# Decode attention with a gated dense branch: key tiles of four heads in 32 KB rows, and a softmax per tile among the key transposes

## The chip, the cores and the metric

One core of a Trainium2 chip. The metric is device time in microseconds, the median of several executions. Engines: PE (matrix products), DVE (VectorE), ACT (ScalarE), POOL (GpSimd), SP (which issues nearly all DMA transfers). "PEclk" is the clock granted to PE, 1.00 being full speed.

## The reference, cut to what matters

One token. Branch A: 32 query heads over 16 key/value heads, a window of 4,096 cached positions, 128 elements per head. Branch B: a dense layer of 576 to 4,608 to 576 with GELU. A sigmoid gate mixes them.

```python
W = min(4096, max(256, Sk // 4))                       # 4096
q = (x @ wq)                                           # 32 heads of 128
k = jnp.repeat(k_cache[:, :, Sk - W:, :], 2, axis=1)   # 16 heads, each for two query heads
v = jnp.repeat(v_cache[:, :, Sk - W:, :], 2, axis=1)
p = softmax(einsum("bhqd,bhkd->bhqk", q, k) * 128**-0.5)
a = einsum("bhqk,bhkd->bhqd", p, v).reshape(1, 1, 4096) @ wo
b = gelu(x @ w1 + b1) @ w2 + b2
return g * a + (1 - g) * b                             # g = sigmoid(sum(x * gate_w))
```

Keys and values are 16.8 MB each and the weights 20.0 MB: 53.6 MB are read once, for one row of output.

## The kernel before

Four large buffers A to D take turns: w1 in B, wq in A, then keys in C, D, B, A, w2 in B, values in C, D, A, C, wo in D. A load can be issued only when the work on its buffer's former content is done, and SP issues in one fixed order. Keys come two heads at a time, in rows of 16 KB (64 blocks of 64 positions x 2 heads = 128 partitions). VectorE transposes them, PE forms the scores of all 16 heads into one tile, then one large softmax runs, then the value products.

```python
s_ps = ps_s.tile([P, SL * 32], FP32, name="s_ps")            # 128 x 2048, all heads
for g in range(NG):                                          # 4 tiles
    k_t = big.tile([P, 2, SL, Dh], BF16, name="k_t", tag="CDBA"[g])
    for f in range(2):                                       # 2 loads each
        h0 = HB * g + 2 * f
        src = A_k_cache[0, h0 : h0 + 2, Sk - W : Sk, :].rearrange(
            "b (k c) d -> k b (c d)", k=P // 2)
        nc.sync.dma_start(out=k_t[:, f, :, :].rearrange("p c d -> p (c d)"), in_=src)
        ...  # two transposes on VectorE, 16 products into s_ps
...  # maximum over everything, two small products, negm
for f in range(2):
    for b in range(HB):
        nc.scalar.activation(out=p_t[:, cs, :, b], in_=..., func=ACT.Exp,
                             bias=negm[:, b : b + 1], scale=SCALE, accum_out=...)
    nc.vector.transpose(out=pt[:, cs, :]..., in_=p_t[:, cs, :, :]...)
w2_t = big.tile([P, NF, D], BF16, name="w2_t", tag="B")
nc.sync.dma_start(out=w2_t[:, 0:NJ, :], in_=w2_src[:, 0])    # first half of w2
...
for g in range(NG):
    v_t = big.tile([P, NCK, Dh], BF16, name="v_t", tag="CDAC"[g])
    nc.sync.dma_start(out=v_t[:].rearrange("p c d -> p (c d)"), in_=src)   # 32 KB rows
    for c in range(NCK):
        v_last = nc.tensor.matmul(o_ps[:, 8 * g : 8 * g + 8, 0], lhsT=v_t[:, c, :], ...)
...  # wo (2 loads), second half of w2 (3 loads), output products, one row out
```

## Time and profile before

| | before |
|---|---|
| time, median of 4 runs | 132.57 us (132.45 to 132.85) |
| span of the profiled run | 131.1 us |
| packets of the data queue, share of 16 DMA engines | 96.3% |
| last weights landed (end of the DMA step in the chain) | 128.24 us |
| from there to the end of the span | 2.9 us |

The bounds are read in the prediction. Two more lines of the page before show the two costliest pieces of work that the change touches (line, engine, operation, output<-input, forms, count; then busy us, mean ns; then idle time before them and who ended it):

```profile
L399 DVE STREAM_TRANSPOSE kt<-k_t 128x2048 f32<-128x2048 f32 x16 | 36.0, 2290 | 6.7 <-DMA k_t<-in_A_k_cache_dram 6.7
L451 ACT ACTIVATE p_t<-s_ps,negm 128x512 bf16<-128x512 f32 x8 | 9.7, 1415 | 44.6 <-DVE negm L442 44.6
```

VectorE idles 6.7 us for keys, so it keeps up with them. ScalarE's softmax is a block of 9.7 us after everything.

### The profile page before, as it was taken

Reading aid. Unit: us, or ns where it says so; the run is one execution under the profiler, and the core shown is the slowest. Engines: PE = TensorE matmul, PEld = TensorE weight load, DVE = VectorE, ACT = ScalarE, POOL = GpSimd, SP = SyncE. Lnnn points to the kernel's source line nnn. Section 1 sums busy time; section 2 is a strip of 40 time slices with the busy share of each in tenths; the row PEclk is TensorE's granted clock in tenths of the full one; section 3 lists DMA queues with packets and bytes.
Section 4 is the critical chain, followed back from the end, with each engine's and each line's share of the span. In section 5 each row is a group of like instructions: output and inputs, shape, how many; then the busy total and the mean of one; then the engine's idle time right before and its main releaser. Section 6 shows DMA issues by size and latency. Waiting matters only on the chain.

```text
span 131.1 us, 2372 instructions
## 1 busy us (share of the span) xinstructions
PE 77.1 (59%) x1126; PEld 44.5 (34%) x1062; DVE 50.3 (38%) x48; ACT 12.9 (10%) x25; POOL 5.9 (4%) x25
## 2 busy tenths in 40 slices
PE   0210899975599968768769220005935740997573
PEld 0110779975111211111111010005834730954441
DVE  0232000042988988988986720735000000010001
ACT  3000000003000000000000039950000000000001
POOL 5029000000000000000000000000000000000000
PEclk9999999999999999999999985555555555558999
DMA  8999899899999999999999999999989999999980
GB/s 290 421 394 496 382 461 421 367 440 420 425 415 440 420 425 435 425 430 425 436 430 489 420 410 450 420 410 450 465 380 435 460 405 392 416 444 415 397 326 20
DMA packets 3044, 53.75 MB, mean 410 GB/s; under 512 B 342, under 2 KB 346, under 8 KB 732
## 3 DMA queue, kind: packets, MB, share of 16 engines
q1 hardware_dynamic: 3026, 53.61, 96.3%
q8 instruction: 8, 0.13, 0.4%
q10 hardware_dynamic: 10, 0.01, 0.0%
HBM read 53.62 MB, written 0.00 MB: 409 GB/s over the span
## 4 chain that ended last, share of the span: by engine, by line
DMA 67%; PE 12%; DVE 8%; ACT 8%; issue 3%; SPq 1%; DVEq 0%
DMA k_t<-in_A_k_cache_dram 26%; DMA w_t<-in_B_w_dram 20%; DMA wq_t<-in_A_wq_dram 20%; ACT p_t L451 7%; PE o_ps L495 5%; DVE kt L399 3%; PE q_ps L356 3%; DVE pt L459 2%; DVE m L421 2%; PE s_ps L409 1%; PE y_ps L291 1%; SPq L508 1%; PE t_ps L475 0%; DVE out_row L537 0%; SPq L510 0%
## 5 line engine op out<-in xcount | busy, mean ns | idle before, releaser
L399 DVE STREAM_TRANSPOSE kt<-k_t 128x2048 f32<-128x2048 f32 x16 | 36.0, 2290 | 6.7 <-DMA k_t<-in_A_k_cache_dram 6.7
L409 PE MATMUL s_ps<-kt,qz_flat 128*128 128x512 bf16 x128 | 32.7, 404 | 8.5 <-DVE kt L399 8.5
L495 PE MATMUL o_ps<-pt,v_t 128*128 128x8 bf16 x512 | 14.5, 168 | 10.4 <-DMA v_t<-in_A_v_cache_dram 7.1
L409 PEld LDWEIGHTS <-qz_flat 128*128 128x128 bf16 x64 | 6.5, 101 | 34.1 <-issue 34.1
L495 PEld LDWEIGHTS <-v_t 128*128 128x128 bf16 x512 | 14.3, 105 | 10.7 <-DMA v_t<-in_A_v_cache_dram 7.3
L451 ACT ACTIVATE p_t<-s_ps,negm 128x512 bf16<-128x512 f32 x8 | 9.7, 1415 | 44.6 <-DVE negm L442 44.6
L318 PEld LDWEIGHTS <-w_t 128*128 128x128 bf16 x162 | 10.2, 165 | 1.0 <-issue 1.0
L318 PE MATMUL h_ps<-x,w_t 128*128 128x2 bf16 x162 | 10.4, 202 | 0.0
L513 DVE TENSOR_TENSOR om<-o_ps,rgh 128x128 bf16<-128x128 f32 x1 | 0.3, 292 | 24.0 <-PE o_ps L495 24.0
L475 PE MATMUL t_ps<-ls,ones 128*128 128x32 f32 x2 | 0.6, 396 | 12.7 <-DVE ls L473 12.7
L459 DVE STREAM_TRANSPOSE pt<-p_t 128x2048 bf16<-128x2048 bf16 x2 | 4.6, 2312 | 7.4 <-ACT p_t L451 7.4
L291 PE MATMUL y_ps<-w_t,gt 128*1 128x288 bf16 x72 | 6.7, 345 | 1.1 <-DMA w_t<-in_B_w_dram 1.1
L327 DVE COPY hacc<-h_ps 128x36 f32<-128x36 f32 x1 | 0.2, 196 | 14.9 <-PE h_ps L318 14.9
L291 PE MATMUL y_ps<-wo_t,ov 128*1 128x288 bf16 x64 | 4.4, 286 | 2.3 <-DMA wo_t<-in_A_wo_dram 2.3
L537 DVE CAST out_row<-y_ps 1x288 bf16<-1x288 f32 x1 | 0.4, 446 | 12.3 <-PE y_ps L291 12.3
L475 PEld LDWEIGHTS t_ps<-ls,ones 128*128 128x128 f32 x2 | 0.5, 310 | 12.8 <-issue 12.8
L291 PEld LDWEIGHTS <-gt 128*1 128x1 bf16 x72 | 3.5, 96 | 3.5 <-issue 1.5
L356 PE MATMUL q_ps<-x,wq_t 128*128 128x2 bf16 x144 | 4.0, 166 | 1.0 <-DMA wq_t<-in_A_wq_dram 1.0
L536 ACT CAST out_row<-y_ps 1x288 bf16<-1x288 f32 x1 | 0.4, 389 | 42.3 <-PE y_ps L291 42.3
L356 PEld LDWEIGHTS <-wq_t 128*128 128x128 bf16 x144 | 3.9, 104 | 1.1 <-DMA wq_t<-in_A_wq_dram 1.1
L291 PEld LDWEIGHTS <-ov 128*1 128x1 bf16 x64 | 2.8, 84 | 3.6 <-issue 2.5
L306 PE MATMUL h_ps<-ident,rows 2*128 2x2 bf16 x18 | 1.3, 198 | 4.2 <-DMA rows<-in_B_b_dram 4.2
(65 smaller groups left out, 27.9 us busy)
## 6 DMA issues: line engine op xcount, KB each, us to landing
k_t<-in_A_k_cache_dram SPq DMA_DIRECT2D x8, 2048.0 KB, 30.4
v_t<-in_A_v_cache_dram SPq DMA_DIRECT2D x4, 4096.0 KB
w_t<-in_B_w_dram SPq DMA_DIRECT2D x1, 4608.0 KB, 14.5
wq_t<-in_A_wq_dram SPq DMA_DIRECT2D x1, 4608.0 KB, 26.0
wo_t<-in_A_wo_dram SPq DMA_DIRECT2D x2, 2304.0 KB, 22.2
w_t<-in_B_w_dram SPq DMA_DIRECT2D x1, 2592.0 KB, 11.3
w_t<-in_B_w_dram SPq DMA_DIRECT2D x1, 1440.0 KB, 25.1
w_t<-in_B_w_dram SPq DMA_DIRECT2D x1, 864.0 KB, 26.8
```

The source lines that it names most:

```text
L291: last = nc.tensor.matmul(y_out[s], lhsT=vec, rhs=row[:, s * DH : (s + 1) * DH], start=start, stop=stop, skip_group_check=True,)
L306: nc.tensor.matmul(h_ps[:, j:NF:NJ], lhsT=b1_t[:, j:FH:NJ], rhs=ident[0:2, 0:2], start=(j == 0), stop=False, skip_group_check=True,)
L318: nc.tensor.matmul(h_ps[:, j:NF:NJ], lhsT=w1_t[:, i, j:FH:NJ], rhs=x2[:, i, :], start=False, stop=(i == NI - 1 and j == NJ - 1), skip_grou ...
L356: nc.tensor.matmul(q_ps[:, j : Hq : Hq // 2], lhsT=wq_t[:, i, j * Dh : (j + 1) * Dh], rhs=x2[:, i, :], start=(i == 0 and j == 0), stop=(i ...
L399: nc.vector.transpose(out=kt[:, u * half : (u + 1) * half].bitcast(FP32), in_=k_t[:, f, u * SL // 2 : (u + 1) * SL // 2, :] .rearrange("p ...
L409: nc.tensor.matmul(s_ps[:, u * 512 : (u + 1) * 512].rearrange("p (c k) -> p c k", k=32), lhsT=qz[:, h0 // 2, j, :], rhs=kv[:, u * SL // 4 ...
L421: nc.vector.reduce_max(out=m2[:], in_=s_ps[:].rearrange("p (n b) -> p b n", b=2), axis=AX.X)
L451: nc.scalar.activation(out=p_t[:, cs, :, b], in_=s_ps[:].rearrange("p (c k u b) -> p u b c k", k=8, u=2, b=2)[:, f, b % 2], func=ACT.Exp, ...
L459: nc.vector.transpose(out=pt[:, cs, :].rearrange("p c h -> p (c h)"), in_=p_t[:, cs, :, :].rearrange("p c k b -> p (c k b)"),)
L475: nc.tensor.matmul(t_ps[:], lhsT=ones[:], rhs=ls[:], start=True, stop=True)
L495: v_last = nc.tensor.matmul(o_ps[:, 8 * g : 8 * g + 8, 0], lhsT=v_t[:, c, :], rhs=pt[:, c, 8 * g : 8 * g + 8], start=(c == 0), stop=(c == ...
L508: nc.sync.dma_start(out=wo_t[:, r0:r1, :], in_=wo_src[:, r0:r1, :])
```

## The change

Its intent: fewer, longer rows of keys, and no block of softmax between keys and values. Each tile of four heads has its own score tile; its maximum, exponentials and transposed probabilities run on VectorE and ScalarE among the key transposes of later tiles, in an order fixed by hand (`queue`). The first value products stand ahead of the last softmax in PE's order, and the first two value loads ahead of w2 in SP's. Four heads share a score tile because positions of foreign heads get -1e30 from two small products per tile.

```diff
-    for i0, i1 in ((0, 1), (1, NI)):
+    for i0, i1 in ((0, 4), (4, NI)):          # first weight load
...
-            src = A_k_cache[0, h0 : h0 + 2, Sk - W : Sk, :].rearrange(
-                "b (k c) d -> k b (c d)", k=P // 2
+        src = cache[0, HB * g : HB * g + HB, Sk - W : Sk, :].rearrange(
+            "b (k c) d -> k b (c d)", k=NKP    # 32 KB rows, keys as values
...
+    transpose(0, 0); scores(0, 0); transpose(0, 1); scores(0, 1)
+    for g in range(1, NG):
+        transpose(g, 0)
+        scores(g, 0)
+        if g > 1:
+            probs(g - 2)
+        row_max(g - 1)
+        transpose(g, 1)
+        scores(g, 1)
+        exps(g - 1)
+    probs(NG - 2)
...
+    v_t = [load("v_t", "CD"[g], A_v_cache, g) for g in range(2)]
     nc.sync.dma_start(out=w2_t[:, 0:NJ, :], in_=w2_src[:, 0])
+    v_t.append(load("v_t", "A", A_v_cache, 2))
...
+    queue("pe", lambda: value_products(0))
+    v_t.append(load("v_t", "C", A_v_cache, 3))
+    row_max(NG - 1)
+    exps(NG - 1)
+    probs(NG - 1)
...
+    queue("pe", lambda: value_products(1))
+    queue("pe", lambda: value_products(2))
...
+    queue("pe", lambda: value_products(3))
```

(The masks, the layout of the query weights and the sums are cut.)

More of the change, by code (lines that the diff above doesn't have):

```diff
@@ L146 @@
     kt_pool = ctx.enter_context(tc.tile_pool(name="kt_pool", bufs=2, side="right"))
-    ps_s = ctx.enter_context(tc.tile_pool(name="ps_s", bufs=1, space=bass.MemoryType.PSUM))
+    ps_s = ctx.enter_context(tc.tile_pool(name="ps_s", bufs=2, space=bass.MemoryType.PSUM))
     ps_y = ctx.enter_context(tc.tile_pool(name="ps_y", bufs=1, space=bass.MemoryType.PSUM))
@@ L176 @@
     nc.gpsimd.memset(one_b[:], 1.0)
-    NCC = 2 * NI + 32 + 4 + 6
+    NCC = 2 * NI + 32 + 4 + 16 + P
     low = const.tile([P, NCC], I32, name="low")
@@ L184 @@
         (128, [[-32, 4]], 96),
-        (8, [[-2, HB]], 6),
-        (4, [[-2, 2]], 2),
+        (128, [[-8, 16]], 120),
+        (128, [[-1, P]], 7),
     ):
@@ L216 @@
     )
-    ident_f = const.tile([P, P], FP32, name="ident_f")
-    nc.gpsimd.tensor_copy(out=ident_f[:], in_=ident[:])
     lo32b = const.tile([P, 32], BF16, name="lo32b")
     nc.gpsimd.tensor_copy(out=lo32b[:], in_=lo32)
-    pens = const.tile([P, HB + 2], FP32, name="pens")
+    c0 = 2 * NI + 36
+    hi16 = const.tile([P, 16], FP32, name="hi16")
     nc.gpsimd.tensor_scalar(
-        out=pens[:],
-        in0=is0[:, 2 * NI + 36 : NCC],
-        scalar1=1e30,
-        scalar2=-1e30,
-        op0=ALU.mult,
-        op1=ALU.add,
-    )
-    pen = pens[:, 0:HB]
-    pen2 = pens[:, HB : HB + 2]
+        out=hi16[:], in0=is0[:, c0 : c0 + 16], scalar1=-SCALE, scalar2=None, op0=ALU.mult
+    )
+    same8 = is0[:, c0 + 16 : NCC]
+    row_of = const.tile([HB, 16, HB, 2], BF16, name="row_of")
+    nc.gpsimd.memset(row_of[:], 0.0)
+    nc.gpsimd.affine_select(
+        out=row_of[:],
+        in_=row_of[:],
+        pattern=[[0, 16], [-1, HB], [0, 2]],
+        compare_op=ALU.not_equal,
+        fill=1.0,
+        base=0,
+        channel_multiplier=1,
+    )
+    foreign = const.tile([HB, P, HB], BF16, name="foreign")
+    nc.gpsimd.memset(foreign[:], -1e30)
+    nc.gpsimd.affine_select(
+        out=foreign[:],
+        in_=foreign[:],
+        pattern=[[0, P], [-1, HB]],
+        compare_op=ALU.not_equal,
+        fill=0.0,
+        base=0,
+        channel_multiplier=1,
+    )
     nc.vector.tensor_copy(
@@ L313 @@
         )
-    qz_flat = const.tile([P, Hkv // 2 * 516 + 128], BF16, name="qz_flat")
+    QZ = 24
+    qz_flat = const.tile([P, QZ + 4 * NG * P + 96], BF16, name="qz_flat")
     nc.gpsimd.memset(qz_flat[:].bitcast(FP32), 0.0)
@@ L365 @@
     nc.scalar.copy(out=q_b[:], in_=q_ps[:])
-    qj_ps = ps_m.tile([P, 4, Hkv // 2, 4], FP32, name="qj_ps", tag="m")
+    qj_ps = ps_m.tile([P, 4, NG, 8], FP32, name="qj_ps", tag="m")
     for j in range(4):
         nc.tensor.matmul(
-            qj_ps[:, j, :, :].rearrange("p s m -> p (s m)"),
+            qj_ps[:, j, :, :].rearrange("p g q -> p (g q)"),
             lhsT=perm[:, j, :, :].rearrange("p b l -> p (b l)"),
@@ L376 @@
         quad = slice(32 * b, 32 * b + 32)
-        diag = qz_flat[quad, 32 * b : 32 * b + Hkv // 2 * 516].rearrange("p (s m) -> p s m", m=516)
+        at = QZ + 32 * b
+        diag = qz_flat[quad, at : at + 4 * NG * P].rearrange(
+            "p (g j m) -> p g j m", g=NG, j=4
+        )
         nc.scalar.copy(
-            out=diag[:, :, 0:512].rearrange("p s (j m) -> p s j m", m=P)[:, :, :, 0:4],
-            in_=qj_ps[quad].rearrange("p j s m -> p s j m"),
-        )
-    qz = qz_flat[:, 0 : Hkv // 2 * 4 * P].rearrange("p (s j m) -> p s j m", s=Hkv // 2, j=4)
@@ L387 @@
-    s_ps = ps_s.tile([P, SL * 32], FP32, name="s_ps")
-    for g in range(NG):
-        k_t = big.tile([P, 2, SL, Dh], BF16, name="k_t", tag="CDBA"[g])
-        for f in range(2):
-            h0 = HB * g + 2 * f
-            src = A_k_cache[0, h0 : h0 + 2, Sk - W : Sk, :].rearrange(
-                "b (k c) d -> k b (c d)", k=P // 2
-            )
-            nc.sync.dma_start(out=k_t[:, f, :, :].rearrange("p c d -> p (c d)"), in_=src)
-            kt = kt_pool.tile([P, SL * Dh], BF16, name="kt", tag="kt")
-            for u in range(2):
-                half = SL * Dh // 2
-                nc.vector.transpose(
-                    out=kt[:, u * half : (u + 1) * half].bitcast(FP32),
-                    in_=k_t[:, f, u * SL // 2 : (u + 1) * SL // 2, :]
-                    .rearrange("p c d -> p (c d)")
-                    .bitcast(FP32),
-                )
-            kv = kt[:].rearrange("p (c e k t) -> p c e k t", e=2, k=32, t=2)
-            for half in range(2):
-                for j in range(4):
-                    for u in (2 * half, 2 * half + 1):
-                        nc.tensor.matmul(
-                            s_ps[:, u * 512 : (u + 1) * 512].rearrange("p (c k) -> p c k", k=32),
-                            lhsT=qz[:, h0 // 2, j, :],
-                            rhs=kv[:, u * SL // 4 : (u + 1) * SL // 4, j // 2, :, j % 2],
-                            start=(h0 == 0 and j == 0),
-                            stop=(h0 == Hkv - 2 and j == 3),
-                            skip_group_check=True,
-                        )
@@ L420 @@
-    m2 = const.tile([P, 2], FP32, name="m2")
-    nc.vector.reduce_max(out=m2[:], in_=s_ps[:].rearrange("p (n b) -> p b n", b=2), axis=AX.X)
-    nc.vector.tensor_tensor(out=m2[:], in0=m2[:], in1=pen2, op=ALU.add)
-    m1 = const.tile([P, 1], FP32, name="m1")
-    nc.vector.reduce_max(out=m1[:], in_=m2[:], axis=AX.X)
-    mt_ps = ps_m.tile([1, P], FP32, name="mt_ps", tag="m")
-    nc.tensor.matmul(mt_ps[:], lhsT=m1[:], rhs=ident_f[:], start=True, stop=True)
-    mh = const.tile([1, 1, Hq], FP32, name="mh")
@@ L428 @@
-    nc.vector.reduce_max(out=mh[:, 0, :], in_=mt_ps[:].rearrange("p (b h) -> p h b", b=4), axis=AX.X)
-    mh4 = const.tile([1, 4, Hq], FP32, name="mh4")
-    nc.vector.tensor_scalar(
-        out=mh4[:],
-        in0=mh[:].to_broadcast([1, 4, Hq]),
-        scalar1=-SCALE,
-        scalar2=None,
-        op0=ALU.mult,
-    )
-    mb_ps = ps_m.tile([P, 1], FP32, name="mb_ps", tag="m")
-    nc.tensor.matmul(
-        mb_ps[:], lhsT=mh4[:].rearrange("p b h -> p (b h)"), rhs=ones[0:1, 0:1], start=True, stop=True
-    )
@@ L441 @@
-    negm = const.tile([P, HB], FP32, name="negm")
-    nc.vector.tensor_tensor(
-        out=negm[:], in0=pen, in1=mb_ps[:].to_broadcast([P, HB]), op=ALU.add
-    )
-    p_t = kt_pool.tile([P, NCK, 8, HB], BF16, name="p_t", tag="kt")
-    pt = kt_pool.tile([P, NCK, Hq], BF16, name="pt", tag="kt")
-    sums = const.tile([P, 2 * HB], FP32, name="sums")
-    for f in range(2):
-        cs = slice(f * SL, (f + 1) * SL)
-        for b in range(HB):
-            nc.scalar.activation(
-                out=p_t[:, cs, :, b],
-                in_=s_ps[:].rearrange("p (c k u b) -> p u b c k", k=8, u=2, b=2)[:, f, b % 2],
-                func=ACT.Exp,
-                bias=negm[:, b : b + 1],
-                scale=SCALE,
-                accum_out=sums[:, f * HB + b : f * HB + b + 1],
-            )
-        nc.vector.transpose(
-            out=pt[:, cs, :].rearrange("p c h -> p (c h)"),
-            in_=p_t[:, cs, :, :].rearrange("p c k b -> p (c k b)"),
-        )
+            out=diag[:, :, :, 0:8],
@@ new lines, with qz @@
+            in_=qj_ps[quad].rearrange("p j g q -> p g j q"),
+        )
+    def qz(g, j, cc):
+        at = QZ + (4 * g + j) * P - 8 * cc
+        return qz_flat[:, at : at + P]
+    m1 = const.tile([P, 1], FP32, name="m1")
+    mr = const.tile([P, 16], FP32, name="mr")
+    negm = const.tile([P, 1], FP32, name="negm")
+    sums = const.tile([P, NG, 1], FP32, name="sums")
+    p_t = const.tile([P, 32, 32], BF16, name="p_t")
+    pt = const.tile([P, NG, 32, 32], BF16, name="pt")
+    mt_ps = ps_m.tile([P, NG * 16 + Hq], FP32, name="mt_ps", tag="m")
@@ new lines, with queue, load @@
+    t_ps = mt_ps[:, NG * 16 : NG * 16 + Hq]
+    issued = {}
+    def queue(engine, emit):
+        if engine in issued:
+            with tc.issue_after(issued[engine].ins):
+                issued[engine] = emit()
+        else:
+            issued[engine] = emit()
+    def load(name, tag, cache, g):
+        tile_ = big.tile([P, NCK, Dh], BF16, name=name, tag=tag)
+        src = cache[0, HB * g : HB * g + HB, Sk - W : Sk, :].rearrange(
+            "b (k c) d -> k b (c d)", k=NKP
+        )
+        nc.sync.dma_start(out=tile_[:].rearrange("p c d -> p (c d)"), in_=src)
+        return tile_
@@ new lines, with transpose @@
+    k_t, s_ps, kt = [None] * NG, [None] * NG, {}
+    def transpose(g, f):
+        if f == 0:
+            k_t[g] = load("k_t", "CDBA"[g], A_k_cache, g)
+        kt[g, f] = kt_pool.tile([P, SL * Dh], BF16, name="kt", tag="kt")
+        keys = k_t[g][:, f * SL : (f + 1) * SL, :]
+        queue(
+            "dve",
+            lambda: nc.vector.transpose(
+                out=kt[g, f][:].bitcast(FP32),
+                in_=keys.rearrange("p c d -> p (c d)").bitcast(FP32),
+            ),
+        )
@@ new lines, in score_products @@
+    def score_products(g, f):
+        if f == 0:
+            for u in range(2):
+                nc.tensor.matmul(
+                    s_ps[g][:, u * 512 : (u + 1) * 512],
+                    lhsT=row_of[:].rearrange("p r b m -> p (r b m)"),
+                    rhs=foreign[:].rearrange("p n b -> p (n b)"),
+                    start=True,
+                    stop=False,
+                    skip_group_check=True,
+                )
+        kv = kt[g, f][:].rearrange("p (c e k t) -> p c e k t", e=2, k=32, t=2)
+        for half in range(2):
+            for j in range(4):
+                for u in range(2):
+                    c0 = (2 * half + u) * SL // 4
+                    last = nc.tensor.matmul(
+                        s_ps[g][:, u * 512 : (u + 1) * 512].rearrange("p (c k) -> p c k", k=32),
+                        lhsT=qz(g, j, 2 * f + half),
+                        rhs=kv[:, c0 : c0 + SL // 4, j // 2, :, j % 2],
+                        start=False,
+                        stop=(f == 1 and half == 1 and j == 3),
+                        skip_group_check=True,
+                    )
+        return last
@@ new lines, in scores, with row_max @@
+    def scores(g, f):
+        if f == 0:
+            s_ps[g] = ps_s.tile([P, 1024], FP32, name="s_ps", tag="s")
+        queue("pe", lambda: score_products(g, f))
+    def row_max(g):
+        queue("dve", lambda: nc.vector.reduce_max(out=m1[:], in_=s_ps[g][:], axis=AX.X))
+        queue(
+            "dve",
+            lambda: nc.vector.tensor_scalar(
+                out=mr[:], in0=hi16[:], scalar1=m1[:, 0:1], scalar2=None, op0=ALU.mult
+            ),
+        )
+        queue(
+            "pe",
+            lambda: nc.tensor.matmul(
+                mt_ps[:, 16 * g : 16 * g + 16], lhsT=same8, rhs=mr[:], start=True, stop=True
+            ),
+        )
@@ new lines, in exps, with probs @@
+    def exps(g):
+        queue(
+            "dve",
+            lambda: nc.vector.tensor_reduce(
+                out=negm[:], in_=mt_ps[:, 16 * g : 16 * g + 16], axis=AX.X, op=ALU.min
+            ),
+        )
+        nc.scalar.activation(
+            out=p_t[:].rearrange("p c k -> p (c k)"),
+            in_=s_ps[g][:],
+            func=ACT.Exp,
+            bias=negm[:, 0:1],
+            scale=SCALE,
+            accum_out=sums[:, g, :],
+        )
+    def probs(g):
+        queue(
+            "dve",
+            lambda: nc.vector.transpose(
+                out=pt[:, g, :, :].rearrange("p c q -> p (c q)"),
+                in_=p_t[:].rearrange("p c k -> p (c k)"),
+            ),
+        )
@@ L465 @@
+    transpose(0, 0)
+    scores(0, 0)
+    transpose(0, 1)
+    scores(0, 1)
+    for g in range(1, NG):
[8 more added lines that the diff above has]
+    probs(NG - 2)
     w2_t = big.tile([P, NF, D], BF16, name="w2_t", tag="B")
     w2_src = B_w2.rearrange("(b p j) n -> p b j n", b=2, j=NJ)
+    v_t = [load("v_t", "CD"[g], A_v_cache, g) for g in range(2)]
@@ L467 @@
     nc.sync.dma_start(out=w2_t[:, 0:NJ, :], in_=w2_src[:, 0])
-    sm = const.tile([P, 1], FP32, name="sm")
-    nc.vector.reduce_sum(out=sm[:], in_=sums[:], axis=AX.X)
-    ls = const.tile([P, Hq], FP32, name="ls")
-    nc.vector.tensor_scalar(out=ls[:], in0=lo32, scalar1=sm[:, 0:1], scalar2=None, op0=ALU.mult)
-    t_ps = ps_m.tile([P, Hq], FP32, name="t_ps", tag="m")
-    nc.tensor.matmul(t_ps[:], lhsT=ones[:], rhs=ls[:], start=True, stop=True)
+    v_t.append(load("v_t", "A", A_v_cache, 2))
@@ new lines, with value_products @@
+    o_ps = ps_m.tile([P, Hq, 1], FP32, name="o_ps", tag="m")
+    def value_products(g):
+        for c in range(NCK):
+            last = nc.tensor.matmul(
+                o_ps[:, 8 * g : 8 * g + 8, 0],
+                lhsT=v_t[g][:, c, :],
+                rhs=pt[:, g, c % 32, 8 * (c // 32) : 8 * (c // 32) + 8],
+                start=(c == 0),
+                stop=(c == NCK - 1),
+            )
+        return last
+    queue("pe", lambda: value_products(0))
+    v_t.append(load("v_t", "C", A_v_cache, 3))
@@ new lines @@
+    row_max(NG - 1)
+    exps(NG - 1)
+    probs(NG - 1)
+    ls = const.tile([P, NG, 8], FP32, name="ls")
+    nc.vector.tensor_tensor(
+        out=ls[:],
+        in0=same8[:, 0:8].rearrange("p (o q) -> p o q", o=1).to_broadcast([P, NG, 8]),
+        in1=sums[:].to_broadcast([P, NG, 8]),
+        op=ALU.mult,
+    )
+    queue("pe", lambda: value_products(1))
+    queue("pe", lambda: value_products(2))
+    queue(
+        "pe",
+        lambda: nc.tensor.matmul(
+            t_ps, lhsT=ones[:], rhs=ls[:].rearrange("p g q -> p (g q)"), start=True, stop=True
+        ),
+    )
@@ L476 @@
     rg = const.tile([P, Hq, 1], FP32, name="rg")
-    nc.vector.reciprocal(out=rg[:, :, 0], in_=t_ps[:])
+    nc.vector.reciprocal(out=rg[:, :, 0], in_=t_ps)
     rgh = const.tile([P, Hq, 4], FP32, name="rgh")
@@ L484 @@
     )
-    o_ps = ps_m.tile([P, Hq, 1], FP32, name="o_ps", tag="m")
-    for g in range(NG):
-        v_t = big.tile([P, NCK, Dh], BF16, name="v_t", tag="CDAC"[g])
-        src = A_v_cache[0, HB * g : HB * g + HB, Sk - W : Sk, :].rearrange(
-            "b (k c) d -> k b (c d)", k=NKP
-        )
-        nc.sync.dma_start(out=v_t[:].rearrange("p c d -> p (c d)"), in_=src)
-        for c in range(NCK):
-            v_last = nc.tensor.matmul(
-                o_ps[:, 8 * g : 8 * g + 8, 0],
-                lhsT=v_t[:, c, :],
-                rhs=pt[:, c, 8 * g : 8 * g + 8],
-                start=(c == 0),
-                stop=(c == NCK - 1),
-            )
+    queue("pe", lambda: value_products(3))
     RO = Hq * Dh // P
@@ L515 @@
     )
-    with tc.issue_after(v_last.ins):
+    with tc.issue_after(issued["pe"].ins):
         for f in range(6):
```

## The prediction

> **What bounds the kernel now.** I read the first page of the profile first: its line of DMA shares over 40 slices of the span, then who is busy.
>
> ```profile
> PE 77.1 (59%) x1126; PEld 44.5 (34%) x1062; DVE 50.3 (38%) x48; ACT 12.9 (10%) x25; POOL 5.9 (4%) x25
> DMA  8999899899999999999999999999989999999980
> HBM read 53.62 MB, written 0.00 MB: 409 GB/s over the span
> ```
>
> No engine is above 59%, while the 16 DMA engines are at eight or nine tenths from the first slice to the last but one. To see whether they ever pause, I cut the span into stages with the view by windows (columns: window and its length, then PE, PEld, DVE, ACT and POOL busy, granted PE clock, DMA share, GB/s).
>
> ```profile
> 36.00:45.00 9.00, 9.00 (x33) 1.71 (x16) 8.10 (x5) 0.00 (x0) 0.00 (x0) 1.00 1.02 430
> 54.00:66.00 12.00, 9.48 (x40) 1.91 (x20) 11.20 (x6) 0.00 (x0) 0.00 (x0) 1.00 1.02 433
> 78.00:90.00 12.00, 0.00 (x0) 0.02 (x1) 4.91 (x4) 9.20 (x16) 0.00 (x0) 0.50 1.00 429
> 102.00:114.00 12.00, 5.84 (x213) 5.67 (x210) 0.00 (x0) 0.00 (x0) 0.00 (x0) 0.50 0.99 421
> 125.00:128.00 3.00, 2.18 (x34) 1.31 (x29) 0.00 (x0) 0.00 (x0) 0.00 (x0) 1.00 0.76 308
> 128.00:131.10 3.10, 1.14 (x16) 0.61 (x15) 0.45 (x1) 0.39 (x1) 0.00 (x0) 1.00 0.04 15
> ```
>
> The third row decides the case. From 78 to 90 us PE does nothing at all: it waits for the one large softmax, which the change wants to break up. Yet the DMA share is 1.00 and 429 GB/s flow. PE's hole costs the transfers nothing. Only the last two rows are below full: a ragged end, then about 2.9 us from the last landing (128.2 us) to the end of the span.
>
> The chain of waits seems to contradict this, for it passes through the softmax (columns: start, length, what).
>
> ```profile
> 66.48 4.52 DVE kt L399 x2
> ...
> 77.53 9.68 ACT p_t L451 x16
> 87.21 0.02 issue
> 87.23 2.31 DVE pt L459
> ...
> 100.97 0.42 SPq L510
> 101.39 0.04 issue
> 101.44 26.80 DMA w_t<-in_B_w_dram
> 128.24 0.04 issue
> 128.28 1.19 PE y_ps L291 x16
> 129.47 0.44 DVE out_row L537
> ```
>
> The catch is the 26.80 us of the last DMA. It is counted from the issue, not from the first byte. The group L495 picks up the last value tile at 111.7 us (timeline), so the queue still had about 10 us of value bytes to move when the last weights were issued at 101.4. Every step of the chain ahead of that issue (keys, softmax, value products) therefore has about 10 us of slack. The bound is bytes over bandwidth plus a fixed head (first byte at about 1.0 us) and a fixed tail (2.9 us).
>
> **What the Trainium skill says.** "DMA: Bandwidth & Descriptors", section "Where 436 GB/s comes from", gives 435.2 GB/s as the ceiling of the fabric and notes 425 for a single core with large transfers. The trace agrees: 421 to 433 GB/s in the stages above, so little is left. The same page, "Why small descriptors are slow (HBM only)", puts the cost of small ones down to a few fixed cycles and 32 bytes of metadata each. That predicts almost nothing for going from 16 KB to 32 KB, and the transfer records agree: a 16,384-byte row took 614 ns (median of 1,032), a 32,768-byte row 1,216 ns (of 512). Again that page, "Anatomy of one DMA — SWDGE (gpsimd) path", says that DMA engines do not wait on semaphores, the issuing sequencer does, ahead of dispatch. So a wait of the SP queue costs time only when it outlasts what is already queued. The trace shows it: SP waited 24.0 us for key tiles at L467 with the DMA share at 1.0. Last, "TensorE: Matmul & The Clock Gate", "What's actually happening", says that an idle PE falls to half clock. The trace agrees: the granted clock is 0.50 from 78 to 119 us, which begins in PE's hole.
>
> **The change part by part.**
>
> (1) *Key rows of 32 KB.* Eight loads of 2 MB become four of 4 MB in the layout that the value tiles have today, so their rows are my measure. A 128-row load puts 8 rows on each of the 16 engines. Before: 64 rows x 0.614 = 39.30 us per engine. After: 32 x 1.216 = 38.91 us. Gain **0.4 us**, on the path. It is at most that: the windows show no higher rate for value tiles (421 to 429 GB/s) than for keys (430 to 433).
>
> (2) *First weight load split 4+5 slices instead of 1+8.* In row medians: before 8 x 0.178 (4,608 bytes) + 8 x 1.364 (36,864) = 12.34 us. After 8 x 0.689 (18,432) + 8 x 0.859 (23,040, an estimate on the line through 774 ns for 20,736 and 1,216 for 32,768) = 12.38 us. Zero, except that the first small rows took 243 ns in the mean, so the ramp lost 8 x 0.065 = 0.5 us; I credit 0.1 us of it, an estimate.
>
> (3) *Scores.* 128 products of 512 columns stay (0.237 us each at full clock: 1.90 us for x8 in the timeline), plus 8 that write the penalty. Packing moves from 128 rows of one tile over 16 heads to one tile per four heads. PE, off the path: +2 us.
>
> (4) *Vector work.* Key transposes: 16 of 2.29 us become 8 of twice the width, 36.6 us both ways. The maximum over 2,048 columns (2.29 us) becomes four over 1,024 (estimate 1.2 each); two transposes of probabilities (2.31) become four of half. So per tile 9.0 + 1.2 + 0.2 + 0.2 + 1.2 = 11.8 us, above the 9.8 us that a key tile takes to arrive. **VectorE falls behind the keys**, and this is the part to work through. Landings from today's records: 36.9, 46.7, 56.6 and 66.4 us for the four tiles (66.4 is in the chain). In the fixed order, transposes of tile 0 end at 45.9; tile 1 at 57.1; tile 2 at about 69; tile 3 at about 81; then scores until 85, the last softmax until about 90. Today the last key transposes end at 71.0, so this is 10 us later.
>
> (5) *What that delay does to the queue.* Each load waits for its buffer. At 9.7 us per value tile and 6.2 us for the first half of w2:
>
> - v0 (after tile 0's transposes) issues at 46, v1 at 57; the queue would run dry at 66.4 and 76.1. The new order, v0 and v1 ahead of w2, matters here.
> - w2's first half (after tile 2) issues at 69, dry at 85.8.
> - v2 (after tile 3) issues at 81, dry at 92.0: **11 us of slack**, the smallest but one.
> - v3 needs the first value products. They follow the last scores (85) and at half clock take 128 x 0.0277 = 3.5 us: issue at about 88.5, dry at 101.7.
> - wo needs the second value products: about 93, dry at 111.4.
>
> The queue never runs dry. Without the new queue order of value products v3 would come some 5 us later, still in time; so that part hides work which was already hidden.
>
> (6) *Softmax.* 9.68 us of ScalarE and the 12.71 us idle of PE ahead of L475 leave the chain. Worth **0**: the transfers did not wait for them. V3's products still start when V3 lands, near 111.4 us, and end near 115; w2's last rows land near 128.
>
> Sum: -0.4 - 0.1 + 0 = -0.5 us at best. I discount it a little, since the window rates show none of it: 132.54 - 0.4 = 132.1 us.
>
> **The rivals.**
>
> *A, the softmax was on the path, as the chain prints it.* Then up to 12 us could go and the time would be 120 to 128. Against it: 429 GB/s during PE's hole, and no fewer bytes; 53.6 MB at 430 GB/s alone are 124.7 us. I give it 2%.
>
> *B, VectorE becomes the bound and starves the queue.* For it: 11.8 us per tile against 9.8. Against it: the slack of 11 us in (5). Should PE also run at half clock in the key stage (0.427 us per product, estimated from the first four of them, 1.58 us), scores end near 99 and v3 issues near 103, 1 to 2 us late: 134 us. Today PE was at full clock from 40 to 78 us with gaps of up to 0.8 us; the new gaps are 1 to 2 us.
>
> *C, the ragged end moves.* Half of the engines end at about 126.4 us, half at about 128. Who carries the last rows can shift by some 0.5 us either way, and the last 16 products at half clock would add about 0.6 us (an estimate: pairs took 0.21 us at clock 0.5 against 0.14 at full).
>
> **Range and chances.** Predicted 132.1 us. Runs of before scatter by 0.4 us; C adds 0.5 either way, and B reaches upward. So 131.5 to 132.8 should hold it 8 times in 10. Two per cent is 2.65 us: faster needs A (0.02), slower needs a dry queue of 3 us (0.02), the same 0.96.
>
> **What would show it.** Right: DMA share near 1.0 and about 425 GB/s in all stages from 3 to 125 us; 32 KB key rows near 1.216 us; the last key transpose ending near 81 us instead of 71, v2 issued near 81, v3 near 88; the last weights landing within 0.7 us of 128.2; PE's hole gone without the end moving. Wrong: a stage between 66 and 112 us with a share below 0.9 (B), the last landing before 127 us (the rows gave more than their medians say), or a tail longer than 3.5 us (C).

## The result, and the profile after

132.37 us (132.32 to 132.50, 4 runs) against 132.57: ratio 0.9983, interval 0.9965 to 1.0000. Two later sets beside the kernel before gave 132.57 against 132.80 (0.9977, 0.9964 to 0.9991) and 132.34 against 132.66 (0.9971, 0.9958 to 0.9983). So the change gains **0.2 to 0.3 us** by the medians (0.2 to 0.4 by the ratios), about a quarter of a per cent. A ratio is the mean time of one kernel's runs over the mean of the other's of the same rounds, so not quite the ratio of the medians.

The same lines of the page after:

```profile
DMA  7999999899899999999999999999989999999980
L441 DVE STREAM_TRANSPOSE kt<-k_t 128x4096 f32<-128x4096 f32 x8 | 35.3, 4432 | 11.8 <-DMA k_t<-in_A_k_cache_dram 10.7
L500 ACT ACTIVATE p_t<-s_ps,negm 128x1024 bf16<-128x1024 f32 x4 | 4.5, 1114 | 50.6 <-DVE negm L496 50.6
```

The DMA line is as full as before. VectorE now idles 10.7 us for keys, all of it ahead of the first tile. The exponentials halved, from 9.7 to 4.5 us: one instruction over 1,024 columns (1,114 ns) is shorter than one over 512 columns was (1,415 ns). Before, their input and output were strided; that this is the reason wasn't tested. In the windows (columns as in the prediction):

```profile
54.00:66.00 12.00, 9.04 (x43) 2.41 (x23) 11.96 (x7) 1.21 (x2) 0.00 (x0) 1.00 1.01 434
78.00:90.00 12.00, 8.97 (x209) 6.18 (x201) 5.89 (x8) 2.41 (x4) 0.00 (x0) 0.83 1.01 431
102.00:114.00 12.00, 6.33 (x221) 6.20 (x219) 0.65 (x2) 0.00 (x0) 0.00 (x0) 0.50 0.97 414
```

PE's hole from 78 to 90 us is filled: 8.97 us busy instead of none. VectorE is at its limit in the key stage, 11.96 of 12 us. And the last two columns, DMA share and GB/s, are what they were (within 0.02 and 7 GB/s). Work was moved beside other work, while the thing that sets the end went on as before.

The chain of waits after (start, length, what) is a warning to its reader:

```profile
79.70 3.62 PE s_ps L463 x16
83.32 3.21 PE o_ps L543 x128
...
93.23 34.61 DMA w_t<-in_B_w_dram
127.84 0.04 issue
127.89 1.19 PE y_ps L306 x16
```

ScalarE is gone from the chain, and VectorE's share rose from 8% to 24%. Yet nothing became faster or slower by it. The one number that moved the end is the landing, 127.84 us instead of 128.24; the tail after it is 2.9 us in both. The last DMA step grew from 26.80 to 34.61 us since it was issued 8 us earlier and only stood longer in the queue.

The times at which SP issued the loads check the prediction's table (part 5). In the timeline of SP (start, length including waits, loads):

```profile
45.83 11.85 SPq L429 DMA_DIRECT2D v_t<-in_A_v_cache_dram  x2
68.41 0.33 SPq L537 DMA_DIRECT2D w_t<-in_B_w_dram  x1
79.66 7.44 SPq L429 DMA_DIRECT2D v_t<-in_A_v_cache_dram  x2
91.91 0.81 SPq L588 DMA_DIRECT2D wo_t<-in_A_wo_dram  x2
```

| load | foretold | issued |
|---|---|---|
| v0, v1 | 46, 57 | 45.8, 57.1 |
| w2, first half | 69 | 68.4 |
| v2, v3 | 81, 88.5 | 79.7, 86.6 |
| wo | 93 | 91.9 |

(A second load of a line is at the end of its stretch less its own 0.54 us.)

### The profile page after: what moved, and what is told of

It is laid out like the page before. It is cut to its first block, busy times and chain, and to the rows that moved or that the text cites. A ratio compares the mean times of both kernels' runs of the same rounds, so it can differ in the third digit from the quotient of the medians.

```text
span 130.7 us, 2382 instructions
## 1 busy us (share of the span) xinstructions
PE 79.9 (61%) x1138; PEld 46.0 (35%) x1071; DVE 51.9 (40%) x47; ACT 8.1 (6%) x17; POOL 8.2 (6%) x28
## 4 chain that ended last, share of the span: by engine, by line
DMA 54%; DVE 24%; PE 13%; issue 6%; SPq 1%; DVEq 0%
DMA k_t<-in_A_k_cache_dram 27%; DMA w_t<-in_B_w_dram 26%; DVE kt L441 19%; PE s_ps L463 7%; PE o_ps L543 5%; DVE m L479 3%; DVE pt L512 2%; PE y_ps L306 1%; SPq L588 1%; DVE mr L482 1%; PE mt_ps L488 0%; DVE out_row L617 0%; SPq L172 0%; SPq L590 0%; SPq L168 0%
## 5 line engine op out<-in xcount | busy, mean ns | idle before, releaser
L441 DVE STREAM_TRANSPOSE kt<-k_t 128x4096 f32<-128x4096 f32 x8 | 35.3, 4432 | 11.8 <-DMA k_t<-in_A_k_cache_dram 10.7
L306 PE MATMUL y_ps<-w_t,gt 128*1 128x288 bf16 x72 | 7.4, 361 | 1.1 <-DMA w_t<-in_B_w_dram 1.1
L500 ACT ACTIVATE p_t<-s_ps,negm 128x1024 bf16<-128x1024 f32 x4 | 4.5, 1114 | 50.6 <-DVE negm L496 50.6
L512 DVE STREAM_TRANSPOSE pt<-p_t 128x1024 bf16<-128x1024 bf16 x4 | 4.9, 1224 | 2.7 <-ACT p_t L500 2.7
L306 PE MATMUL y_ps<-wo_t,ov 128*1 128x288 bf16 x64 | 4.9, 299 | 1.4 <-DMA wo_t<-in_A_wo_dram 1.4
L343 DVE COPY hacc<-h_ps 128x36 f32<-128x36 f32 x1 | 0.2, 196 | 13.2 <-PE h_ps L334 13.2
L479 DVE TENSOR_REDUCE m<-s_ps 128x1 f32<-128x1024 f32 x4 | 4.8, 1196 | 1.1 <-PE s_ps L463 1.1
L255 PE MATMUL xs_ps<-one_b,rows 1*128 1x1 bf16 x9 | 0.7, 196 | 7.2 <-DVE rows L249 7.2
L249 DVE COPY rows<-rows 1x1152 bf16<-1x1152 bf16 x1 | 0.7, 748 | 6.4 <-DMA rows<-in_A_x_dram 6.4
```

The lines of the kernel that those rows point to most:

```text
L249: nc.vector.tensor_copy(out=xdup.rearrange("p (d t) -> p d t", t=2), in_=x_row.rearrange("p (d o) -> p d o", o=1).to_broadcast([1, D, 2]),)
L306: last = nc.tensor.matmul(y_out[s], lhsT=vec, rhs=row[:, s * DH : (s + 1) * DH], start=start, stop=stop, skip_group_check=True,)
L441: lambda: nc.vector.transpose(out=kt[g, f][:].bitcast(FP32), in_=keys.rearrange("p c d -> p (c d)").bitcast(FP32),),
L479: queue("dve", lambda: nc.vector.reduce_max(out=m1[:], in_=s_ps[g][:], axis=AX.X))
L500: nc.scalar.activation(out=p_t[:].rearrange("p c k -> p (c k)"), in_=s_ps[g][:], func=ACT.Exp, bias=negm[:, 0:1], scale=SCALE, accum_out=s ...
L512: lambda: nc.vector.transpose(out=pt[:, g, :, :].rearrange("p c q -> p (c q)"), in_=p_t[:].rearrange("p c k -> p (c k)"),),
```

## The experiments

The theory: transfers bound the kernel from end to end; the long rows are the whole gain; the new softmax order moves only slack. Rivals: the softmax was on the path (A), VectorE is now the bound (B), the gain comes from the first load or the new order. Runs of one set share their runs of the kernel before. Names that begin with a_ are variants of the changed kernel, with b_ of the kernel before.

### Set 1: which part gives the gain

**The changed kernel again.**

> The changed kernel again, beside its variants. Both theories: 132.3 to 132.5 us, 0.1 to 0.3 us under the kernel before.

Measured: 132.57 us against 132.80, ratio 0.9977.

**16 KB rows in the changed kernel.**

```diff
-        nc.sync.dma_start(out=tile_[:].rearrange("p c d -> p (c d)"), in_=src)
+        flat = tile_[:].rearrange("p c d -> p (c d)")
+        n = NCK * Dh
+        parts = 2 if name == "k_t" else 1
+        for s in range(parts):
+            at = slice(s * n // parts, (s + 1) * n // parts)
+            nc.sync.dma_start(out=flat[:, at], in_=src[:, :, at])
```

> The changed kernel with every key tile loaded by two transfers of 16 KB rows; all else as in the changed kernel. Theory (the transfers bound the kernel, and the 32 KB rows are the whole gain): back to the time of before, 132.6 to 132.8 us, 0.3 to 0.4 us over the changed kernel, last weights landing 0.3 us later. Rival (the gain comes from the new softmax order or the first weight load): it stays at the changed kernel's time.

Measured: 133.02 us, ratio 1.0019 (1.0006 to 1.0033) to the kernel before, so 0.45 us over the changed kernel of the same rounds and 0.2 over the kernel before (and over the foretold range). The records of single transfers in the traces agree: the median of a 16,384-byte row is 614 ns and that of a 32,768-byte row 1,216 ns in every trace here that has them, so 32 rows saved 32 x (2 x 614 - 1,216) = 0.38 us per DMA engine. Summed over all rows of the data queue, a DMA engine was busy for 126.11 us in the kernel before, 126.16 in this variant and 125.75 in the changed kernel of the same set. So the gain is the rows, and without them the change would be a loss of about 0.2 us, which isn't in the row times. The profiled run of this variant, the slowest of its six (133.38 us), has one more effect: its last output products ran in part at half clock (see "Fewer rows elsewhere"). I can't say how much of the 0.2 us that is.

**The first load's split alone, in the kernel before** (`((0, 1), (1, NI))` becomes `((0, 4), (4, NI))`).

> The kernel before with only the first weight load split 4+5 slices instead of 1+8. Theory: no change, 132.5 us within 0.1. Rival (the smoother start is the gain): 132.2 to 132.35 us.

Measured: 132.81 against 132.80 us, ratio 0.9995 (0.9980 to 1.0009). Nothing. The loss at the start isn't due to short rows: in the changed kernel the 384 rows of 18,432 bytes have a median of 689 ns but a mean of 722, since the very first ones are slow whatever their length. Over its median rows the first load lost 0.6 us per DMA engine in the kernel before, and 0.7 (this variant) to 0.8 us (the changed kernel) with the new split.

**Fewer rows elsewhere.**

```diff
-    for i0, i1 in ((0, 4), (4, NI)):
+    for i0, i1 in ((0, NI),):
-    for r0, r1 in ((0, 16), (16, RO)):
+    for r0, r1 in ((0, RO),):
-    for j0, j1 in ((0, 10), (10, 16), (16, 18)):
+    for j0, j1 in ((0, 12), (12, 18)):
```

> The changed kernel with fewer, longer rows elsewhere too: first weights in one load (41,472 bytes a row), output weights in one (36,864), the second half of w2 in two loads instead of three. Theory: every row costs about 12 ns on top of its bytes, so 8 x 3 rows fewer per engine save 0.3 us and the last group of products starts with fewer to do: 132.0 to 132.2 us, under both kernels. If rows cost nothing, or the later arrival of the first pieces matters: 132.4 us or more.

Measured: 133.82 us (132.93 to 134.65), ratio 1.0082 (1.0047 to 1.0117): a miss, with a wide spread. The last row did arrive earlier (127.92 us against 128.22 in the records), but PE was late in the run that was profiled (133.63 us). PE's timeline of this variant, from the landing of the output weights on (idle time before, and who ended it, in brackets):

```profile
122.20 5.39 PE L306 MATMUL y_ps<-wo_t,ov 128*1 128x288 bf16 x58 [2.11 <-DMA wo_t<-in_A_wo_dram]
127.42 1.39 PE L306 MATMUL y_ps<-w_t,gt 128*1 128x288 bf16 x20
```

and the same stretch of the changed kernel in that set:

```profile
122.39 2.74 PE L306 MATMUL y_ps<-wo_t,ov 128*1 128x288 bf16 x42 [1.47 <-DMA wo_t<-in_A_wo_dram]
125.86 1.39 PE L306 MATMUL y_ps<-w_t,gt 128*1 128x288 bf16 x20 [0.72 <-DMA w_t<-in_B_w_dram]
```

The lower one waits for a transfer before each of these groups, and again for 0.36 us before its last at 127.97. The upper one never waits after 122.2 us: its last group starts at 129.01, and PE is the bound of its tail. It had 16 more products to do there (100 against 84), and from 124 to 126 us the granted clock was 0.50 against 1.00. The three pieces of w2 and the two of wo, which looked like waste, keep PE's work small after each landing.

### Set 2: was the softmax on the path, and what did the new order buy

**Half of the exponentials left out, in the kernel before** (a wrong result).

```diff
+    nc.gpsimd.memset(sums[:], 0.0)
...
-        for b in range(HB):
+        for b in range(HB if f == 0 else 0):
...
-            in_=p_t[:, cs, :, :].rearrange("p c k b -> p (c k b)"),
+            in_=p_t[:, 0:SL, :, :].rearrange("p c k b -> p (c k b)"),
```

> The kernel before with the second four of the eight exponentials left out, the first four used twice (wrong result on purpose): the large softmax is 4.7 us shorter. Theory (transfers bound, softmax has some 8 us of slack): no change, 132.5 us within 0.2. Rival A (the chain of waits is right that the softmax is on the path): about 128 us.

Measured: 132.75 against 132.62 us, ratio 1.0020 (0.9994 to 1.0045). No gain. The test is weaker than I expected: the softmax lost 4.7 us of exponentials, but its two transposes, the first of which had been hidden behind the exponentials, now follow them one after the other, so the value products began only 2.0 us earlier (88.44 us instead of 90.43). On the path that would still have shown as 2 us, so rival A falls. In its chain of waits the output weights were issued earlier and stood in the queue for just so much longer:

```profile
99.69 28.42 DMA w_t<-in_B_w_dram
```

1.75 us earlier in the queue (99.69 instead of 101.44), 1.62 us longer in it (28.42 instead of 26.80).

**12 us of needless VectorE work ahead of the softmax, in the kernel before.**

```diff
+    held = mh4_op                       # the instruction that scales the maximum
+    for _ in range(10):
+        with tc.issue_after(held.ins):
+            held = nc.vector.transpose(out=spare[:, 1, :], in_=spare[:, 0, :])
+    with tc.issue_after(held.ins):
         nc.vector.tensor_tensor(
             out=negm[:], in0=pen, in1=mb_ps[:].to_broadcast([P, HB]), op=ALU.add
         )
```

> The kernel before with ten needless transposes (12 us of VectorE) ahead of the bias of its softmax. Theory: the fourth value load, issued at 94.0 us, moves to about 106 while the queue runs dry at 99 to 101, so 5.5 to 7.5 us are lost: 138 to 140 us. Rival (softmax on the path): 144.5 us. If nothing depended on it: 132.5.

Measured: 141.30 us, ratio 1.0651 (1.0629 to 1.0672), a loss of 8.7 us. The direction is the theory's, the size isn't: I had allowed for 5.5 to 7.5. The windows of this variant show an empty queue:

```profile
99.00:101.00 2.00, 0.00 (x0) 0.00 (x0) 1.57 (x1) 0.40 (x2) 0.00 (x0) 0.50 0.23 98
101.00:103.00 2.00, 0.79 (x15) 0.82 (x16) 1.17 (x4) 0.00 (x0) 0.00 (x0) 0.50 0.00 0
```

Ten of the 16 DMA engines ended their last row at 99.4 to 99.8 us, the rest by 101.3. The fourth value load was issued at 106.24, but its first rows began at 107.6 on half of the engines and at 108.4 on the rest, and took up to 2.1 us instead of 1.22. **A dry queue costs more than the wait**: here about 1.3 us to start, and slow first rows.

**The same 12 us ahead of the last softmax of the changed kernel** (ten such transposes ahead of `row_max(NG - 1)`).

> The changed kernel with the same ten transposes ahead of its last softmax. Theory: the fourth value load no longer waits for the last softmax, and the output weights, issued at 91.9, move to about 103 with the queue dry only at 109 to 111: no change, 132.4 us within 0.2. So the change bought slack that this kernel doesn't use. Rival: it loses like the kernel before.

Measured: 132.24 us, ratio 0.9969 (0.9952 to 0.9985): free. The delay is there, and PE works on meanwhile:

```profile
82.08 12.72 DVE L428 STREAM_TRANSPOSE spare<-spare 128x1024 bf16<-128x1024 bf16 x10
83.04 3.36 PE L549 MATMUL o_ps<-pt,v_t 128*128 128x8 bf16 x128
```

The first value products run at 83 us, beside the delay, and free the buffer of the fourth value load. So with value products ahead of the last softmax the kernel bears a late softmax that costs the kernel before 8.7 us. That is what the reordering bought, together with the softmax per tile, which lets value products start before the last tile's probabilities exist; the two weren't tested apart. The kernel has no use for it as it is.

**The queue order of before (first half of w2 ahead of the first value tiles), in the changed kernel.**

```diff
-    v_t = [load("v_t", "CD"[g], A_v_cache, g) for g in range(2)]
-    nc.sync.dma_start(out=w2_t[:, 0:NJ, :], in_=w2_src[:, 0])
+    w2_first = nc.sync.dma_start(out=w2_t[:, 0:NJ, :], in_=w2_src[:, 0])
+    with tc.issue_after(w2_first.ins):
+        v_t = [load("v_t", "CD"[g], A_v_cache, g) for g in range(2)]
```

> The changed kernel with the queue order of before: the first half of w2 ahead of the first two value tiles. It then waits for the third key tile's transposes (68.4 us) while the keys end at 64 to 65.5 us. Theory: the queue runs dry for 3.5 to 5.5 us, 136 to 138 us. If the order doesn't matter: 132.4.

Measured: 139.20 us, ratio 1.0497 (1.0449 to 1.0546), 1.2 us over the foretold range. Windows of this variant:

```profile
62.00:64.00 2.00, 2.00 (x10) 0.48 (x5) 2.00 (x2) 0.00 (x0) 0.00 (x0) 1.00 0.65 279
66.00:68.00 2.00, 0.00 (x0) 0.00 (x0) 2.00 (x1) 0.00 (x0) 0.00 (x0) 1.00 0.00 0
```

From 66 to 68 us nothing moves while VectorE still transposes the third key tile, whose buffer w2 needs. The load was issued at 68.75 us and its first row began at 69.72; first rows took up to 2.3 us instead of 0.77. So this line of the diff isn't an improvement; it is what keeps the rest of the change from costing 6.6 us (139.20 - 132.62), because VectorE now lags behind the keys.

### Set 3: how much slack VectorE has left

Needless transposes (1.28 us from one to the next in the traces) ahead of the last key transpose of the changed kernel, six and eighteen:

```diff
         row_max(g - 1)
+        if g == NG - 1:
+            idle_work(6)                # 18 in the second
         transpose(g, 1)
```

> The changed kernel with six needless transposes (7.2 us of VectorE) ahead of the last key transpose. Theory: the third value load, issued at 79.7 us, moves to about 87, and the queue runs dry at 90 to 91.5: no change, 132.4 us within 0.2. Rival B (VectorE is the bound by now): about 139.6 us.

Measured: 133.53 us (132.57 to 134.13) against 132.78, ratio 1.0038 (0.9985 to 1.0091): the same as the kernel before within the noise, but 1.1 us over the 132.4 us foretold, to which the changed kernel itself kept within 0.2 us in its three sets. The third value load was issued at 88.05 us, 8.4 us later than in the changed kernel. The DMA engines came to the end of their rows at 89.3 to 91.1 us, and the first rows of the new load, which began at 89.38, took up to 2.1 us. The last row of all ended at 129.05 us instead of 128.12. So the slack is used up at about 8 us, not 11.

> The same with eighteen transposes (21.7 us). Theory: the third value load moves to about 101.4 us, 10 to 12 us after the queue ran dry: 142 to 145 us, so that about half of the added work shows. Rival B: 154 us.

Measured: 146.09 us, ratio 1.0998 (1.0961 to 1.1035), a loss of 13.3 us and 1 us over the foretold range. The load was issued at 102.25 us. One thing other than the delay changed: the scheduler put a piece of the second half of w2 ahead (at 68.5 us), so the queue drained at 92.8 to 94.5, and the second half of the output weights landed only at 136.93. In its chain of waits follows:

```profile
136.97 5.35 PE y_ps L306 x84
```

84 products ran behind this landing without a wait, 5.35 us, where the changed kernel had 16 and 1.19 us left at its last one. The last rows of w2 arrived meanwhile, at 139.34 us against 128.12 in the changed kernel (11.2 us later); from there the span ran on for 4.6 us instead of 2.6. The gap in the queue (about 11 us) and 2 us of this tail make up the loss. That VectorE is not the bound (rival B) holds, since 23 us of added work cost 13; but the reading is not a clean one.

### Set 4: the fewer rows again, with the output weights back in two loads

> The kernel with fewer rows, but the output weights again in two loads as in the changed kernel. In the earlier run the last landing moved 0.3 us forward as foretold, yet 84 of the last 100 products ran after one late landing of the output weights (122.2 us), in part at half clock, and PE ended the kernel. Theory: with the first half of the output weights back at about 120 us, PE is done with them in time and the end follows the last landing again: 132.2 to 132.5 us, 0.1 to 0.2 under the changed kernel. If it stays near 133.8, the merged output weights were not the cause.

Measured: 132.93 against 132.66 us, ratio 1.0015 (1.0004 to 1.0027), against 0.9971 for the changed kernel in the same rounds: a second miss, though it is 0.27 us over the kernel before where the first was 1.02 over it. The merged output weights were the larger part of that loss. PE's timeline of this variant suggests the rest:

```profile
126.35 1.39 PE L306 MATMUL y_ps<-w_t,gt 128*1 128x288 bf16 x20 [1.42 <-DMA w_t<-in_B_w_dram]
```

The larger first piece of w2 lets PE start its last 42 products at 126.35 us; no transfer interrupts them, and they end at 129.35. The changed kernel of the same set started them at 125.66 and ended at 128.92, with one more wait for a transfer (0.36 us) between. The earlier arrival is also smaller than foretold: the last row ended at 127.97 us against 128.04. The pieces of w1 and w2 weren't tested apart. No version beat the changed kernel.

> The changed kernel beside it in the same rounds: ratio to the kernel before 0.9977 to 0.9983 again.

Measured: 132.34 us, ratio 0.9971 (0.9958 to 0.9983).

## Why the prediction was right

The time alone proves little: the range, 131.5 to 132.8 us, also holds the kernel before (132.57). What counts are the parts.

- **The bound.** Right. Softmax work taken away (half of the exponentials) changed nothing, and the DMA share stayed near 1 in all stages after.
- **Part 1, key rows, -0.4 us.** Right in cause and near in size: 0.45 us lost when the rows alone were undone, 0.38 us by the row records of the changed kernel, 0.40 us at the last landing. (The 1,032 rows of 16,384 bytes include the eight instruction fetches of that size; the median isn't touched.)
- **Part 2, first load, -0.1 us.** Wrong. The split alone gives 0.0 us; the slow first rows are slow at any length.
- **Part 4, VectorE falls behind.** Right: 11.96 of 12 us busy, the last key transpose over at 79.6 us where 81 was foretold. The transposes took 4.43 us instead of twice 2.29.
- **Part 5, the queue doesn't run dry.** Right, with every issue within 2 us of the table. The step that failed is its slack of 11 us. It measured about 8, since I counted from the last key landing (66.4 us) to one moment, 92.0 us. The engines ran out of rows one by one from 89.3 to 91.1 us (six needless transposes), and a new load needs 1.3 us from the start of its issue to its first row: 89.3 - 1.3 - 79.7 = 8.3. Also, 11 us was not "the smallest but one" of the slacks in the list but the smallest (v3 has 101.7 - 88.5 = 13.2). The remark that the order of v0 and v1 ahead of w2 "matters here" was right, by 6.6 us.
- **Part 6, the softmax is worth 0.** Right in what it says of the time. Not foretold, the block softmax in the kernel before had so little slack that 12 us more cost 8.7, and the change takes this away. So the working that gave every step of the old chain "about 10 us of slack" failed there: it looked at the issue of the last weights (101.4 us), but the softmax also holds back the fourth value load, issued at 94.0 us, and for that load the delayed run left only about 4 us (its first engine was out of rows at 99.4 us, less 1.3 for the start).
- **Rival C, the clock at the end.** It came true in variants only: from 124 to 126 us the granted clock was 0.50 in the profiled runs with 16 KB rows and with fewer rows, 1.00 in the changed kernel.
- **Rival B's half clock.** 0.427 us per product doesn't follow from 1.58 us for four, which is 0.395. The weight loads there, one per two products, came 0.85 us apart, which does give it. In the changed kernel PE was at half clock from 68.9 to 72.3 us in the key stage, and no load came late by it.
- **The sum.** -0.4 us foretold, -0.2 to -0.3 measured (medians) in three sets. Part 2's 0.1 us is missing. In the 16 KB variant the other parts together cost about 0.2 us (133.02 against 132.80), which would account for the rest; which of them does is open.

## What to carry to other kernels

When the DMA engines are full from end to end, a hole in another engine is not a cost, and a chain of waits that runs through it only shows how long a load stood in the queue: subtract that time before believing in the chain. A reordering that fills such a hole buys slack, which is worth time only if something else would use it. What must be checked in such a change is the time of every load's issue against the time at which the queue runs dry, with a margin for the restart, and how much work is left after each of the last landings.

## What the Trainium skill lacked or had wrong

- "DMA: Bandwidth & Descriptors", section "Latency and other measured facts", gives about 0.6 us to the first byte for loads issued from SP, without saying from when it counts, and nothing on a restart. After a dry queue the first row began 0.97 us after the start of the issue with 20,736-byte rows (0.64 after its end) and 1.34 us after it with 32,768-byte rows (0.80 after its end; two runs). In these two runs half of the engines began another 0.6 to 0.8 us later, and first rows took up to 2.1 us instead of 1.22. The page has no time per long row either: 614 ns for 16,384 bytes and 1,216 ns for 32,768, so about 12 ns on top of the bytes, and 0.38 us of 132 in this kernel.
- "Runtime: NRT & Kernel Launch", section "Instruction fetch mechanics", says that fetches come in blocks of 16 KiB and are mostly hidden. It has no time for one. In the kernel before, each of the 8 fetches of 16 KB took 1.0 to 1.1 us (a data row of that size takes 0.61), and with the fetch counted 15 or 16 transfers were in flight, no more than without it, so it took a data row's turn on a DMA engine. Half of the DMA engines ended some 1.5 us after the others. PE may have felt a fetch too: it paused for 2.49 us at 94.84 us with no recorded cause, and a fetch began at 94.8. Neither link was tested.
- No page has it that the cut of the last loads sets what PE has left to do after each landing: with one load of the output weights instead of two, PE had 100 products left after their landing instead of 84, and the kernel (with two other loads merged too) took 1.0 us more than the kernel before.
